# RWKV-7 recurrence with a gated mixture of experts: chunks of 64 steps on two diagonal 64x64 blocks of the array, in place of chunks of 128 steps

## The chip, the cores and the metric

One NeuronCore of one Trainium2 chip runs the kernel. The metric is the device time in microseconds (us), the median of several runs; a profiled execution of the same program gives the trace. TensorE's granted clock is shown by the trace as a share of full speed: 1.00 is 2.4 GHz and 0.50 is 1.2 GHz.

## The reference, cut to what matters

```python
# r, k, v, w, a, b: (4 batches, 8 heads, 768 steps, 40), float32
for t in range(S):                       # 768 steps, one after the other
    y[:, :, t] = einsum('bhd,bhde->bhe', rt, state)
    Sa = einsum('bhde,bhe->bhd', state, at)
    state = state * wt[:, :, None, :] - outer(Sa, bt) + outer(vt, kt)
x = y as (3072 tokens, 320)              # 4 x 768 tokens, 8 heads x 40
# two-level gate: argmax of 4 groups, then of 4 experts in the group
# out[token] = gate weight * (relu(x @ w1[expert]) @ w2[expert])
# w1: 16 experts of 320 x 1024; w2: 16 experts of 1024 x 320
```

## The kernel before, in words

The kernel has three stages. The recurrence makes the tokens (L157 to L376). The gate (L452 to L598) ranks the tokens by expert. The expert network (L601 to L681) gathers the tokens of each of 16 experts, multiplies by both weight matrices and scatters the result.

The recurrence cuts the 768 steps into 6 chunks of 128. A **unit** (L192) is one chunk of one batch with all 8 heads, so there are 24 units. Heads lie in pairs: the 40 rows of an even head on partitions 0 to 39, those of an odd head on partitions 64 to 103 (`blk`, L189). Within a unit the decay products are scanned (L218), inverted (L222) and multiplied into a, b and k (L224 to L226). `product` (L236) makes the 128x128 matrices GT, E, MT and NT of each head from 40-row operands; `natural` (L228) transposes on TensorE. The solve with the unit triangular matrix I+E runs in 7 levels (L281): in each, E and its transpose are squared for each head (L287, L296; 128x128 weights, 128 columns), and the 40 columns of U are multiplied (L307; 128x128 weights, 40 columns). ScalarE and VectorE copy each result from PSUM (L290, L300, L302, L313). Then follow the new state (L328 to L332, L356), the output (L342 to L351), its transpose and the gate logits (L135, L146).

Everything is float32. A matmul call on float32 stands in the trace as two records, each with a weight load of its own. The instructions of each engine run in the order that a list scheduler writes at build time: it takes the earliest instruction in program order whose inputs and buffers are ready, by its own cost table, so that work of the next unit is put where an earlier one waits. Inputs are held in three buffers (`NB = 3`). PSUM has five slots of one bank ("big") and three ("small"). A guard at the end (L368 to L379) sets the trip count of a step-by-step loop, which is zero here. Two expert weight buffers are filled during the recurrence (`WE = 2`), and a third exists from the expert stage on.

Of the kernel before, what the change touches and what calls it, by code (L numbers as in the profile page):

```python
# [9 lines left out]
F32 = mybir.dt.float32  # L10
# [11 lines left out]
W_MIN, W_MAX, T_MAX = 0.765, 1.3, 1.0  # L22
# [3 lines left out]
def kernel(  # L26
# [19 lines left out]
    C = P  # L46
    NC = S // C
    NN = B * NC
    NP = H // 2
    HW = 64  # L50
# [13 lines left out]
    LEVELS = C.bit_length() - 1  # L64
# [7 lines left out]
    psum = ctx.enter_context(tc.tile_pool(name="ps", bufs=1, space=PSUM))  # L72

    def big(shape):
        return psum.tile(shape, F32, tag="big", name="big", bufs=5)

    def small(shape):
        return psum.tile(shape, F32, tag="small", name="small", bufs=3)
# [13 lines left out]
    up4 = up[:, None, :].broadcast_to([P, NP, P])  # L92
    low4 = low[:, None, :].broadcast_to([P, NP, P])

# [3 lines left out]
    wg = cpool.tile([P, NK, NW], F32, name="wg")  # L98
    for ko, (k0, kn) in enumerate(KO):
        nc.scalar.dma_start(out=wg[:kn, ko, :G], in_=w_group[k0:k0 + kn, :])  # L100
        nc.scalar.dma_start(out=wg[:kn, ko, G:].rearrange("p (g e) -> p g e", g=G),
                            in_=w_expert[:, k0:k0 + kn, :].rearrange("g p e -> p g e"))
# [3 lines left out]
    WE = 2  # L106
# [20 lines left out]
    t_sum = cpool.tile([P, NN, H], F32, name="t_sum")  # L127
    w_max = cpool.tile([P, NN], F32, name="w_max")
    w_min = cpool.tile([P, NN], F32, name="w_min")
# [11 lines left out]

    def gate_logits(pool, xn, n):
        t = transpose_x(pool, xn)
        ps = small([P, NW])
        for ko, (_, kn) in enumerate(KO):
            nc.tensor.matmul(ps, lhsT=t[:kn, ko, :], rhs=wg[:kn, ko, :],  # L146
                             start=(ko == 0), stop=(ko == NK - 1))
        nc.scalar.copy(out=lg[:, n, :], in_=ps)

    with ExitStack() as part:  # L157
        pers = part.enter_context(tc.tile_pool(name="pers", bufs=1))
        sb = part.enter_context(tc.tile_pool(name="sb", bufs=2))

        NB = 3
        ins = []
        for i in range(NB):
            d = {}
            for nm in "wakbvr":
                d[nm] = pers.tile([P, NP, C], F32, name=f"in_{nm}{i}")
            d["pq"] = pers.tile([P, NP, C + 1], F32, name=f"pq{i}")
            ins.append(d)
        zeros = pers.tile([P, C], F32, name="zeros")
        nc.vector.memset(zeros, 0.0)  # L170
        U_pad = []
        for i in range(2):
            t = pers.tile([P, H, HW], F32, name=f"U{i}")
            nc.gpsimd.memset(t[:, :, D:], 0.0)
            U_pad.append(t)


        ST, SN = [], []
        for b_ in range(B):
            t = pers.tile([P, NP, 2, HW], F32, name=f"ST{b_}")  # L180
            nc.gpsimd.memset(t, 0.0)
            ST.append(t)
            SN.append(pers.tile([P, NP, 2, HW], F32, name=f"SN{b_}"))
        own = pers.tile([P, 2], F32, name="own")
        nc.gpsimd.memset(own, 0.0)
        for j in range(2):
            nc.gpsimd.memset(own[j * HW:(j + 1) * HW, j:j + 1], 1.0)

        def blk(h):  # L189
            return slice((h % 2) * HW, (h % 2) * HW + D)  # L190

        for u in range(NN):  # L192
            c, b_ = divmod(u, B)
            n = b_ * NC + c
            t0 = c * C
            d = ins[u % NB]
            if u < NB:

                for nm in "wakbvr":
                    for q0 in (32, 96):  # L200
                        nc.any.memset(d[nm][q0:q0 + 32], 1.0 if nm == "w" else 0.0)  # L201
                nc.any.memset(d["pq"][:, :, 0:1], 1.0)
            if NB < u <= NB + WE:
                load_weights(u - NB - 1, wbuf[u - NB - 1])
            for nm, src in (("w", wT), ("a", aT), ("b", bT), ("k", kT), ("r", rT), ("v", vT)):
                sv = src[b_, :, :, t0:t0 + C].rearrange("(i j) d t -> j d i t", j=2)
                for j in range(2):
                    nc.sync.dma_start(out=d[nm][j * HW:j * HW + D], in_=sv[j])
            vn = sb.tile([P, H, D], F32, name="vn")
            nc.sync.dma_start(out=vn, in_=v[b_, :, t0:t0 + C, :].rearrange("h t d -> t h d"))  # L210


            nc.vector.tensor_reduce(out=w_max[:, n:n + 1], in_=d["w"], axis=AX.XY, op=ALU.max)
            nc.vector.tensor_reduce(out=w_min[:, n:n + 1], in_=d["w"], axis=AX.XY, op=ALU.min)
            nc.vector.tensor_scalar(d["w"], d["w"], W_MIN, W_MAX, op0=ALU.max, op1=ALU.min)
            pq = d["pq"]
            for i in range(NP):
                nc.vector.tensor_tensor_scan(pq[:, i, 1:], d["w"][:, i, :], zeros, 1.0,  # L218
                                             op0=ALU.mult, op1=ALU.add)
            Pm, Qm = pq[:, :, :C], pq[:, :, 1:]  # L220
            Qi = d["w"]
            nc.vector.reciprocal(out=Qi, in_=Qm)  # L222
            At, Kt, Bt, Rt, Vt = d["a"], d["k"], d["b"], d["r"], d["v"]
            nc.vector.tensor_tensor(At, At, Pm, op=ALU.mult)  # L224
            nc.gpsimd.tensor_tensor(Bt, Bt, Qi, op=ALU.mult)
            nc.gpsimd.tensor_tensor(Kt, Kt, Qi, op=ALU.mult)  # L226

            def natural(src, name, scale):  # L228
                pt = big([P, NP, P])
                for i in range(NP):  # L230
                    nc.tensor.transpose(pt[:, i, :], src[:, i, :], ident)
                t = sb.tile([P, NP, P], F32, name=name)
                nc.scalar.mul(t, pt, scale)
                return t

            def product(lhs, rhs, g, mask, name, bufs):  # L236
                ps = big([P, NP, P])
                for q in range(NP):
                    nc.tensor.matmul(ps[:, q, :], lhsT=lhs[blk(g), q, :], rhs=rhs[blk(g), q, :],  # L239
                                     start=True, stop=True)  # L240
                t = sb.tile([P, NP, P], F32, name=name, bufs=bufs)
                nc.vector.tensor_tensor(t, ps, mask, op=ALU.mult)  # L242
                return t


            GR = range(2)
            GT = [product(Kt, At, g, up4, "GT", 4) for g in GR]

            E = [product(At, Bt, g, low4, "E", 6) for g in GR]
            ET = []  # L250
            for g in GR:
                ts = t_sum[:, n, g * NP:(g + 1) * NP]
                nc.vector.tensor_reduce(out=ts, in_=E[g], axis=AX.X, op=ALU.add,
                                        apply_absolute_value=True)
                fit = sb.tile([P, NP, 1], F32, name="fit")
                nc.vector.tensor_scalar(fit[:, :, 0], ts, T_MAX, None, op0=ALU.max)  # L256
                nc.vector.reciprocal(out=fit, in_=fit)
                nc.gpsimd.tensor_tensor(E[g], E[g], fit.broadcast_to([P, NP, P]), op=ALU.mult)  # L258
                pt = big([P, NP, P])
                for i in range(NP):  # L260
                    nc.tensor.transpose(pt[:, i, :], E[g][:, i, :], ident)
                t = sb.tile([P, NP, P], F32, name="ET", bufs=6)
                nc.scalar.copy(out=t, in_=pt)
                ET.append(t)
            MT = [product(Vt, Rt, g, up4, "MT", 4) for g in GR]
            nB = natural(Bt, "nB", -1.0)
            Kn = natural(Kt, "Kn", 1.0)
            Pn = natural(Pm, "Pn", 1.0)


            ps = small([P, H, D])
            for i in range(NP):
                if c:
                    nc.tensor.matmul(ps[:, 2 * i:2 * i + 2, :], lhsT=At[:, i, :],
                                     rhs=ST[b_][:, i, :, :D], start=True, stop=False)
                for j in range(2):
                    nc.tensor.matmul(ps[:, 2 * i + j, :], lhsT=GT[j][:, i, :], rhs=vn[:, 2 * i + j, :],  # L277
                                     start=(c == 0), stop=(c == 0 or j == 1))
            U = sb.tile([P, H, D], F32, name="U", bufs=3)
            nc.scalar.copy(out=U, in_=ps)  # L280
            for lv in range(LEVELS):  # L281
                if lv:
                    E2, ET2 = [], []
                    for g in GR:
# [7 lines left out]
                        if lv == LEVELS - 1:  # L292
                            continue
# [415 lines left out]
```

## Time and profile before

| | us |
|---|---|
| median of 3 runs (2051.61 to 2067.24) | 2060.82 |
| the profiled execution: its own time | 2059.22 |
| its span, first to last instruction | 2057.5 |
| its mean granted TensorE clock | 0.795 |
| VectorE busy in the span | 635.0 |
| ScalarE busy in the span | 411.5 |

The span is read in stages: a lead-in without a matmul, the recurrence, the gate, the experts. PE is the matmul queue and PEld its weight loads, DVE is VectorE, ACT ScalarE, POOL GpSimd, SP the queue that issues most transfers. A matmul record of shape 128*128 has weights of 128 rows and 128 columns; "128x40" behind it is the operand that streams, 128 rows and 40 columns. The ends of matmul records are modelled, so the distance between starts is the better price.

### The profile page before, as it was taken

The page shows a single profiled execution, that of the slowest core. Times are in us where ns is not written, and L with a number is a line of the kernel's source. Part 1 is how long each engine was busy: PE and PEld are TensorE (multiplying, and loading weights), DVE is VectorE, ACT ScalarE, POOL GpSimd, SP SyncE. Part 2 cuts the span into 40 slices and gives each one's busy share as a digit, 9 for nine tenths or more (in the row PEclk, how much of TensorE's full clock was granted, in tenths as well). Part 3 has the DMA queues.
Part 4 walks back from the last instruction along what each step waited for, and adds up shares of the span by engine and source line. Part 5 has one row for each costly group of instructions (what it writes and reads, how often), then busy time and mean ns, then how long its engine had stood idle before and what let it go on. Part 6 is the DMA issues. An engine that isn't in the chain of part 4 may idle for free. (4 is left out here: it accounts for less than half of the span.)

```text
span 2057.5 us, 29577 instructions
## 1 busy us (share of the span) xinstructions
PE 1942.0 (94%) x12542; PEld 1820.6 (88%) x12542; DVE 635.0 (31%) x1113; ACT 411.5 (20%) x755; POOL 194.7 (9%) x196
## 2 busy tenths in 40 slices
PE   5999999999999999999999999999999937999997
PEld 5999999999999999999999999999999936777776
DVE  8433332332334233323332333233221251111111
ACT  3122222212222122122221221122112200000000
POOL 3000000000000000000000000000000002121210
PEclk9787788758878688588786886687677858999999
DMA  5200000000000000000000000000000003444430
GB/s 142 64 20 20 26 23 14 17 26 16 18 20 27 15 22 17 27 18 18 17 26 20 17 17 23 14 20 17 10 4 1 4 5 133 153 160 153 159 128 11
DMA packets 104553, 84.59 MB, mean 41 GB/s; under 512 B 31961, under 2 KB 97502, under 8 KB 104416
## 3 DMA queue, kind: packets, MB, share of 16 engines
q1 hardware_dynamic: 99648, 73.42, 11.9%
q0 software_dynamic: 3072, 9.18, 1.1%
q8 instruction: 102, 1.67, 0.3%
q10 hardware_dynamic: 1696, 0.03, 0.0%
q14 instruction: 35, 0.29, 0.0%
HBM read 74.74 MB, written 9.18 MB: 41 GB/s over the span
## 5 line engine op out<-in xcount | busy, mean ns | idle before, releaser
L307 PE MATMUL small<-U,ET 128*128 128x40 f32 x2688 | 345.9, 290 | 0.6 <-ACT ET L290 0.4
L307 PEld LDWEIGHTS small<-U,ET 128*128 128x128 f32 x2688 | 341.1, 205 | 2.3 <-ACT ET L290 0.5
L287 PE MATMUL big<-ET,E 128*128 128x128 f32 x2304 | 335.8, 292 | 0.1
L287 PEld LDWEIGHTS big<-ET,E 128*128 128x128 f32 x2304 | 299.7, 203 | 0.2 <-DVE E L302 0.2
L296 PE MATMUL big<-E,ET 128*128 128x128 f32 x1920 | 265.8, 284 | 0.0
L290 ACT COPY ET<-big 128x512 f32<-128x512 f32 x288 | 168.7, 586 | 481.3 <-PE big L287 481.3
L296 PEld LDWEIGHTS big<-E,ET 128*128 128x128 f32 x1920 | 247.1, 201 | 0.0
L313 DVE TENSOR_TENSOR U<-U,small 128x320 f32<-128x320 f32 x168 | 80.7, 480 | 457.5 <-PE small L307 457.5
L633 PE MATMUL big<-xT,w1s 128*128 128x256 f32 x768 | 171.4, 383 | 10.3 <-DVE xT L626 10.3
L633 PEld LDWEIGHTS big<-xT,w1s 128*128 128x128 f32 x768 | 145.6, 191 | 34.2 <-DVE xT L626 14.8
L258 POOL TENSOR_TENSOR E<-E,fit 128x512 f32<-128x512 f32 x48 | 48.9, 1039 | 1189.5 <-DVE fit L256 1137.8
L642 PE MATMUL small<-w2s,hT 128*128 128x320 f32 x512 | 140.4, 432 | 0.0
L642 PEld LDWEIGHTS small<-w2s,hT 128*128 128x128 f32 x512 | 97.3, 190 | 38.8
L239 PE MATMUL big<-in_a,in_k 40*128 40x128 f32 x384 | 89.0, 447 | 17.1 <-DVE in_b L201 17.1
L348 PE MATMUL small<-nB,NT 128*128 128x40 f32 x384 | 100.2, 356 | 0.0
L239 PEld LDWEIGHTS big<-in_a,in_k 40*128 40x128 f32 x384 | 75.1, 322 | 26.9 <-POOL in_k L226 17.1
L302 DVE COPY E<-big 128x512 f32<-128x512 f32 x96 | 66.2, 691 | 100.1 <-PE big L296 98.5
L346 PE MATMUL small<-Kn,MT 128*128 128x40 f32 x384 | 96.0, 344 | 0.0
L300 ACT COPY E<-big 128x512 f32<-128x512 f32 x144 | 84.3, 585 | 50.4 <-PE big L296 50.4
L277 PE MATMUL small<-vn,GT 128*128 128x40 f32 x384 | 94.1, 402 | 0.0
L277 PEld LDWEIGHTS small<-vn,GT 128*128 128x128 f32 x384 | 91.8, 333 | 0.9 <-DVE E L242 0.7
L348 PEld LDWEIGHTS small<-nB,NT 128*128 128x128 f32 x384 | 87.7, 281 | 2.3 <-DVE NT L242 2.3
(189 smaller groups left out, 2064.2 us busy)
## 6 DMA issues: line engine op xcount, KB each, us to landing
w2s<-in_w_dram SPq DMA_DIRECT2D x16, 1280.0 KB
w1s<-in_w_dram SPq DMA_DIRECT2D x16, 1024.0 KB
w1s<-in_w_dram SPq DMA_DIRECT2D x16, 256.0 KB
vn<-in_v_dram SPq DMA_DIRECT2D x24, 160.0 KB
in_w<-in_wT_dram SPq DMA_DIRECT2D x48, 80.0 KB
in_a<-in_aT_dram SPq DMA_DIRECT2D x48, 80.0 KB
in_b<-in_bT_dram SPq DMA_DIRECT2D x48, 80.0 KB
in_k<-in_kT_dram SPq DMA_DIRECT2D x48, 80.0 KB
```

What stands on the lines that cost most here:

```text
L239: nc.tensor.matmul(ps[:, q, :], lhsT=lhs[blk(g), q, :], rhs=rhs[blk(g), q, :], start=True, stop=True)
L277: nc.tensor.matmul(ps[:, 2 * i + j, :], lhsT=GT[j][:, i, :], rhs=vn[:, 2 * i + j, :], start=(c == 0), stop=(c == 0 or j == 1))
L287: nc.tensor.matmul(ps[:, q, :], lhsT=E[g][:, q, :], rhs=ET[g][:, q, :], start=True, stop=True)
L290: nc.scalar.copy(out=t, in_=ps)
L296: nc.tensor.matmul(ps[:, q, :], lhsT=ET[g][:, q, :], rhs=E[g][:, q, :], start=True, stop=True)
L300: nc.scalar.copy(out=t, in_=ps)
L307: nc.tensor.matmul(ps[:, h, :], lhsT=ET[h % 2][:, h // 2, :], rhs=U[:, h, :], start=True, stop=True)
L313: nc.vector.tensor_tensor(nx, U, ps, op=ALU.add if lv else ALU.subtract)
L346: nc.tensor.matmul(o, lhsT=MT[j][:, i, :], rhs=Kn[:, i, blk(j)], start=(c == 0), stop=False)
L348: nc.tensor.matmul(o, lhsT=NTm[j][:, i, :], rhs=nB[:, i, blk(j)], start=False, stop=(c == 0 or j == 1))
L633: nc.tensor.matmul(ps[:, f, :], lhsT=w1s[:, ko, (f0 + f) * P:(f0 + f + 1) * P], rhs=xT[:, ko, :w], start=(ko == 0), stop=(ko == NK - 1))
L642: nc.tensor.matmul(ps, lhsT=hT[:, f, t_ * P:(t_ + 1) * P], rhs=w2s[:, f, :], start=(f == 0), stop=(f == FQ - 1))
```

## The change

The recurrence is rewritten; the gate and the experts stay. A unit is now one chunk of 128 steps of two batches (12 units), and each unit holds two chunks of 64 steps (24 chunks), one after the other. A chunk treats 8 head pairs (`NI`) at once. Each matmul of a chunk uses a 64x64 block of the array: rows and columns 0 to 63 for an even head, 64 to 127 for an odd head, issued in turn (`each`). Both heads of a pair write the same PSUM bank, on partitions 0 to 63 and 64 to 127. There are 6 levels in place of 7; they form the inverse itself (`ED`'s right half, then `DT`) and no longer carry U. U is then DT times the right-hand side. The state is updated every 64 steps and scaled by the decay product every 128. The output is formed transposed (`yT`). The decay scan runs over four head pairs at once, the reciprocal over 8. PSUM is cut into two "wide" slots of two banks and four slots of one bank. Two sums of squares on ScalarE take the place of the clamp of w in the guard. Input buffers are two (`NB = 2`, each of twice the size), and one expert weight buffer is filled early (`WE = 1`).

Left out of the diff below, in the order of the program, calls of a chunk, each on a 64x64 block with 64 columns or fewer: 16 for E (At by Bt), 16 for MT (Vt by Rt); in level 0, 16 for ED's left half and 16 for the square of E; in level 4, 16 for ED's right half and 16 for the square; in level 5, 16 for DT; after the right-hand side (RHS) 16 for U (DT by RHS), 32 for the state (GK by vn, TBt by U), 16 each for UT, NTm and Sn. At the end of a unit stand, for each of its two batches, 4 transposes of yT and 4 gate matmuls with yT as weights, all with 128x128 weights.

```diff
+    HW = P // 2
+    L = 2 * HW
+    NS = 2
+    BS = B // NS
+    NI = BS * NP
-    LEVELS = C.bit_length() - 1
+    LEVELS = HW.bit_length() - 1
-    WE = 2
+    WE = 1
...
+            return psum.tile([P, NI, 2 * HW], F32, tag="wide", name="wide", bufs=2)
...
+            for i in range(NI):
+                for j in range(2):
+                    yield i, j
...
+            nc.vector.reciprocal(out=Qi, in_=pq[:, :, 1:])
+            junk = sb.tile([P, NI, L + 1], F32, name="junk", bufs=1)
+            nc.scalar.activation(junk, pq, ACT.Square, accum_out=q_sum[:, 2 * u:2 * u + 1])
...
+                for lhs, out_t, mask in ((Kt, GK, m_gk), (Bt, TBt, m_tb)):
+                    ps = wide()
+                    for i, j in each():
+                        nc.tensor.matmul(ps[half(j), i, :HW + D], lhsT=lhs[half(j, D), i, ts],
+                                         rhs=At[half(j, D), i, c2, :HW + D], start=True, stop=True)
+                    nc.vector.tensor_tensor(out_t[:, :, :HW + D], ps[:, :, :HW + D], over(mask),
+                                            op=ALU.mult)
...
+                for lv in range(LEVELS):
...
+                    elif lv < LEVELS - 2:
+                        ps = wide()
+                        for i, j in each():
+                            nc.tensor.matmul(ps[half(j), i, :], lhsT=E[half(j), i, :],
+                                             rhs=ED[half(j), i, :], start=True, stop=True)
+                        nxt = sb.tile([P, NI, 2 * HW], F32, name="ED", bufs=3)
+                        nc.scalar.copy(out=nxt[:, :, :HW], in_=ps[:, :, :HW])
+                        nc.vector.tensor_tensor(nxt[:, :, HW:], ps[:, :, HW:], ED[:, :, HW:], op=ALU.add)
...
+                    if not last:
+                        ps = bank([P, NI, HW], "one", 2)
+                        for i, j in each():
+                            nc.tensor.matmul(ps[half(j), i, :], lhsT=ET[half(j), i, :],
+                                             rhs=E[half(j), i, :], start=True, stop=True)
+                        E = sb.tile([P, NI, HW], F32, name="E", bufs=3)
+                        nc.scalar.copy(out=E, in_=ps)
...
+                ps = bank([P, NI, D], "seq", 2)
+                for i, j in each():
+                    nc.tensor.matmul(ps[half(j), i, :], lhsT=GK[half(j), i, :HW], rhs=vn[half(j), c2, i, :],
+                                     start=True, stop=fresh)
+                    if not fresh:
+                        nc.tensor.matmul(ps[half(j), i, :], lhsT=At[half(j, D), i, c2, :HW],
+                                         rhs=S0[half(j, D), i, :D], start=False, stop=True)
+                nc.scalar.copy(out=RHS[:, :, :D], in_=ps)
...
+                ps = bank([P, NI, HW], "one", 2)
+                for i, j in each():
+                    if not fresh:
+                        nc.tensor.matmul(ps[half(j), i, :], lhsT=Sn[half(j, D), i, :],
+                                         rhs=Rt[half(j, D), i, ts], start=True, stop=False)
+                    nc.tensor.matmul(ps[half(j), i, :], lhsT=GK[half(j), i, HW:], rhs=MT[half(j), i, :],
+                                     start=fresh, stop=False)
+                    nc.tensor.matmul(ps[half(j), i, :], lhsT=TBt[half(j), i, HW:], rhs=NTm[half(j), i, :],
+                                     start=False, stop=True)
+                nc.vector.tensor_tensor(yT[:, :, ts], ps, Pm[:, :, ts], op=ALU.mult)
```

## Rows read from the trace of the kernel before

**Rows 1.** The page: busy time of each engine; granted clock in 40 slices.
```profile
PE 1942.0 (94%) x12542; PEld 1820.6 (88%) x12542; DVE 635.0 (31%) x1113; ACT 411.5 (20%) x755; POOL 194.7 (9%) x196
PEclk9787788758878688588786886687677858999999
```

**Rows 2.** Windows by stage; columns PE, PEld, DVE, ACT, POOL busy, clock, DMA share, GB/s.
```profile
0.00:17.08 17.08, 0.00 (x1) 0.00 (x1) 14.26 (x24) 12.55 (x20) 9.53 (x25) 1.00 0.50 124
...
400.00:1600.00 1200.00, 1176.90 (x8134) 1139.21 (x8133) 377.46 (x642) 267.99 (x484) 78.77 (x64) 0.75 0.07 18
...
1660.50:1717.85 57.35, 15.95 (x70) 12.56 (x70) 25.79 (x75) 1.49 (x7) 9.74 (x16) 0.56 0.18 61
```

**Rows 3.** Windows between four changes of the granted clock; columns as in Rows 2.
```profile
740.00:768.38 28.38, 27.62 (x245) 27.00 (x243) 6.12 (x13) 7.92 (x14) 0.00 (x0) 1.00 0.04 7
768.38:788.86 20.48, 20.07 (x101) 18.64 (x102) 7.00 (x16) 3.22 (x7) 2.04 (x2) 0.50 0.12 36
788.86:822.99 34.13, 33.55 (x301) 33.40 (x300) 13.70 (x20) 11.14 (x20) 2.94 (x2) 1.00 0.05 13
822.99:867.37 44.38, 43.80 (x216) 41.85 (x215) 15.88 (x26) 6.47 (x13) 4.98 (x4) 0.50 0.11 29
```

**Rows 4.** Timeline at clock 1.00: start, duration, engine, line, operands, shapes, count.
```profile
803.17 1.06 PE L287 MATMUL big<-ET,E 128*128 128x128 f32 x8
...
804.06 1.06 PE L296 MATMUL big<-E,ET 128*128 128x128 f32 x8
...
804.95 1.88 PE L307 MATMUL small<-U,ET 128*128 128x40 f32 x16
...
806.66 1.14 PE L287 MATMUL big<-ET,E 128*128 128x128 f32 x8
```

**Rows 5.** Timeline at clock 0.50, two row blocks in turn.
```profile
773.41 0.42 PE L239 MATMUL big<-in_a,in_k 40*128 40x128 f32 x1
...
773.57 0.42 PE L239 MATMUL big<-in_b,in_a 40*128 40x128 f32 x1
...
773.62 0.42 PE L239 MATMUL big<-in_a,in_k 40*128 40x128 f32 x1
...
773.79 0.42 PE L239 MATMUL big<-in_b,in_a 40*128 40x128 f32 x1
...
773.83 0.42 PE L239 MATMUL big<-in_a,in_k 40*128 40x128 f32 x1
```

**Rows 6.** Timeline at clock 0.50, full blocks with few columns, 24 records in all.
```profile
776.22 0.71 PE L274 MATMUL small<-ST,in_a 128*128 128x80 f32 x2
776.73 0.99 PE L277 MATMUL small<-vn,GT 128*128 128x40 f32 x4
...
781.36 1.95 PE L261 MATMUL big<-ident,E 128*128 128x128 f32 x8
```

**Rows 7.** Groups by line and shape: busy us, mean ns of one | idle before.
```profile
L307 PE MATMUL small<-U,ET 128*128 128x40 f32 x2688 | 345.9, 290 | 0.6 <-ACT ET L290 0.4
...
L624 PEld LDWEIGHTS big<-ident,xt 128*128 128x128 f32 x64 | 8.6, 145 | 13.1 <-issue 9.1 <-DMA xt<-x_nat,src_i 0.9
...
L624 PEld LDWEIGHTS big<-ident,xt 128*64 128x64 f32 x32 | 3.7, 115 | 0.0
```

**Rows 8.** Groups by line and shape, other engines.
```profile
L290 ACT COPY ET<-big 128x512 f32<-128x512 f32 x288 | 168.7, 586 | 481.3 <-PE big L287 481.3
...
L222 DVE RECIPROCAL in_w<-pq 128x512 f32<-128x512 f32 x24 | 80.5, 3353 | 0.8
...
L226 POOL TENSOR_TENSOR in_k<-in_k,in_w 128x512 f32<-128x512 f32 x24 | 39.5, 1648 | 0.0
```

**Rows 9.** Timelines: two matmuls that wait for a copy, idle time in brackets.
```profile
759.66 0.66 PE L318 MATMUL big<-ident,U 128*128 128x128 f32 x4 [0.58 <-DVE U L313]
...
1649.31 3.09 PE L239 MATMUL big<-in_r,UT 40*128 40x128 f32 x16 [0.68 <-ACT UT L321]
```

**Rows 10.** Window in which an expert's weights land; columns as in Rows 2.
```profile
1710.00:1720.00 10.00, 3.93 (x11) 2.70 (x12) 0.85 (x2) 0.52 (x2) 4.82 (x6) 0.52 0.92 322
```

More of the change, by code (lines that the diff above doesn't have):

```diff
@@ L16 @@
 DRAM = bass.MemoryType.DRAM
-W_MIN, W_MAX, T_MAX = 0.765, 1.3, 1.0
+Q_MAX, T_MAX = 1e30, 1.0
 @with_exitstack
@@ L45 @@
     DM = H * D
-    C = P
-    NC = S // C
+    HW = P // 2
+    L = 2 * HW
+    NC = S // L
+    NP = H // 2
+    NS = 2
+    BS = B // NS
+    NI = BS * NP
+    CH = NS * NC * 2
     NN = B * NC
-    NP = H // 2
-    HW = 64
     G, Eg = w1.shape[0], w1.shape[1]
@@ L71 @@
     dpool = ctx.enter_context(tc.tile_pool(name="dram", bufs=1, space=DRAM))
[L72 to L78, printed above, removed]
     ident = cpool.tile([P, P], F32, name="ident")
@@ L91 @@
                             pattern=[[-1, P]], channel_multiplier=1)
-    up4 = up[:, None, :].broadcast_to([P, NP, P])
-    low4 = low[:, None, :].broadcast_to([P, NP, P])
     x_nat = dpool.tile([NTOK, DM], F32, name="x_nat")
     lg = cpool.tile([P, NN, NW], F32, name="lg")
[L98 to L102, printed above, removed]
-    WE = 2
+    wgp = cpool.tile([P, NP, NW], F32, name="wgp")
+    nc.gpsimd.memset(wgp, 0.0)
+    for j in range(2):
+        rows = slice(j * HW, j * HW + D)
+        nc.scalar.dma_start(out=wgp[rows, :, :G],
+                            in_=w_group.rearrange("(i j d) g -> j d i g", j=2, d=D)[j])
+        for g in range(G):
+            nc.scalar.dma_start(out=wgp[rows, :, G + g * Eg:G + (g + 1) * Eg],
+                                in_=w_expert[g].rearrange("(i j d) e -> j d i e", j=2, d=D)[j])
+    WE = 1
     KR = KO[-1][1]
@@ L131, in transpose_x, with big, small @@
+    psum = ctx.enter_context(tc.tile_pool(name="ps", bufs=1, space=PSUM))
+    def big(shape):
+        return psum.tile(shape, F32, tag="big", name="big", bufs=5)
+    def small(shape):
+        return psum.tile(shape, F32, tag="small", name="small", bufs=3)
     def transpose_x(pool, src):
@@ L444 @@
         with tc.For_i(0, n_back, 1):
+            wg = sq.tile([P, NK, NW], F32, name="wg")
+            for ko, (k0, kn) in enumerate(KO):
+                nc.scalar.dma_start(out=wg[:kn, ko, :G], in_=w_group[k0:k0 + kn, :])
+                nc.scalar.dma_start(out=wg[:kn, ko, G:].rearrange("p (g e) -> p g e", g=G),
+                                    in_=w_expert[:, k0:k0 + kn, :].rearrange("g p e -> p g e"))
             for n in range(NN):
@@ L447 @@
                 nc.sync.dma_start(out=xn, in_=x_nat[n * P:(n + 1) * P, :])
-                gate_logits(sq, xn, n)
+                t = transpose_x(sq, xn)
+                ps = small([P, NW])
+                for ko, (_, kn) in enumerate(KO):
+                    nc.tensor.matmul(ps, lhsT=t[:kn, ko, :], rhs=wg[:kn, ko, :],
+                                     start=(ko == 0), stop=(ko == NK - 1))
+                nc.scalar.copy(out=lg[:, n, :], in_=ps)
     with ExitStack() as part:
```

419 lines of the change are left out of this document (209 added, 210 removed).

## The prediction

> **What bounds the kernel now.** I read the page first. TensorE is busy 94% of the span, VectorE 31%, ScalarE 20% [rows 1]. The windows by stage say where: in the 1200 us from 400 on, TensorE is busy 1177, so only 2% is idle, at a mean granted clock of 0.75 [rows 2]. So the recurrence is bound by TensorE's own records; nearly every wait of the other engines is cover. The lead-in without a matmul takes 17.08 us, and gate and experts take 2057.5 - 1660.5 = 397 us, of which only the first weights change [rows 2].
>
> The mean clock of 0.75 hides two levels. From 740 to 768.38 us the clock stands at 1.00, then 20.5 us at 0.50, 34.1 at 1.00, 44.4 at 0.50 [rows 3]. TensorE is busy in all of them (20.07 of 20.48, 43.80 of 44.38), so a busy engine alone doesn't hold the clock up. What differs is what it does: at 1.00 it streams full 128x128 blocks, most of them with 128 columns [rows 4]; in the 0.50 stretches lie the 40-row products [rows 5] and full blocks that stream only 40 or 80 columns [rows 6].
>
> Three prices come from distances between starts. At 1.00, 8 records with 128 columns take 0.89 us, 111 ns each, and 16 records with 40 columns take 1.71 us, 107 ns each [rows 4]. So with 128 weight columns, few streamed columns save nothing. At 0.50, 24 records with 40 or 80 columns take 5.14 us, 214 ns each [rows 6]. And two products on different row blocks, issued in turn, overlap: starts at 773.41, 773.57, 773.62, 773.79, 773.83 are two records per 0.21 us at 0.50, the time of one [rows 5].
>
> **The change part by part.** One old unit and one new chunk are the same share of the work, 24 of each. A call is two records 8 heads x 7 levels x 24 units x 2 = 2688 [rows 7]. When calls alternate between the two blocks, the second record of one runs beside the first of the next, so a call costs one step. I take the clock at 0.50 (reasons below).
>
> The price of a 64-column step isn't in the trace. It lies between 107 ns at 0.50, half of the 128-column step, and 214 ns, no saving. The nearest row: a weight load of 64 columns takes 115 ns where one of 128 takes 145 [rows 7], 30 ns less for 64 columns, which is about a column per 2.4 GHz clock. So I take the proportional price: 107 ns up to 64 columns, 174 for 104, 214 for 128.
>
> A chunk then has:
> - GK and TB: 32 calls with 104 columns, 5.6 us.
> - Levels 1 to 3, the double-width products: 48 calls with 128 columns, 10.3 us.
> - Calls with at most 64 columns that alternate (E, MT, the other level products, DT, U, UT, NTm, Sn): 224 x 107 ns = 24.0 us.
> - Groups in which the calls of one head follow each other on the same block: RHS and state, 64 calls, three steps for two; y, 48 calls, five steps for three. 96 + 80 = 176 steps, 18.8 us.
> - Transposes and gate calls: 16 calls, 32 records of 214 ns per unit, 3.4 us per chunk.
>
> That is 62.1 us, times 24 = 1490; two chunks without state save 17 us and the last two, without a state update, 10: **1463 us**. What it removes is the old 1643 us from 17.08 to 1660.5.
>
> Idle time comes on top. A chunk has 11 hand-offs in which TensorE needs a copy of what it has just made: E, five squares, DT, RHS, U, UT, NTm. Uncovered, one costs 0.58 to 0.68 us [rows 9], so 7.5 us per chunk, 180 in all. One reciprocal over 1024 columns blocks VectorE's queue for 2 x 3.35 = 6.7 us [rows 8], and the level's add behind it, for which TensorE waits: 12 x 6.7 = 80. With nothing covered the recurrence takes 1463 + 260 = 1723; covered as now (2% idle) 1463 / 0.98 = 1493. The next chunk's GK, TB, E and MT (9 us) need nothing from the levels and can cover them, but two wide and two single PSUM slots serve both. I take a quarter of the way, **1550**.
>
> ScalarE's copies (13 per chunk) of at most 586 ns [rows 8], about 8 us, hide beside 62 us of TensorE, and so do the two sums of squares; were ScalarE the bound, the recurrence would take under 300 us.
>
> The lead-in grows: the reciprocal doubles (+3.35) and so does the product with k on GpSimd (+1.65) [rows 8], and the scans; 17 becomes 23. The last chunk's end has no next chunk to cover it: +10. A unit's loads (2240 KB, 18 us at the lead-in's 124 GB/s [rows 2]) queue on SP, and behind them the stores of x; with two input buffers they have a whole unit, over 120 us, to land: nothing. If that cover failed, each unit would pay up to 18 us. `WE = 1` moves one expert's load (2.56 MB, 8 us at the 322 GB/s of [rows 10]) into the time of expert 0, 339.65 / 16 = 21 us: nothing; without that cover 8 us per expert.
>
> Sum: 23 + 1550 + 10 + 397 = 1980 of span. The profiled execution takes 1.7 us more than its span (2059.22 against 2057.5), and the median is 1.6 above that run: I forecast **1982 us**. A 1% difference, some 20 us, is about what a measurement of this kernel can tell from none.
>
> **Why the half clock.** In the stretches at 1.00 full 128x128 blocks prevail; two 64x64 blocks together fill half of its cells, with the 40-row operands less. The nearest rows are the 40-row pairs [rows 5]: two blocks overlap, the engine doesn't pause, and the clock stays at 0.50. But those blocks have all 128 columns and few rows, the new ones 64 of each; the trace has no stretch of blocks with half the columns, so whether unused columns count like unused rows is open.
>
> The Trainium skill, TensorE: Matmul & The Clock Gate, Part 1, says that a busy engine releases the throttle and an idle one brings it back. By that rule the new recurrence would run at 1.00, which is the first rival below; the trace speaks against the plain rule, since the engine is busy 43.80 of 44.38 us at 0.50.
>
> **The rivals.**
> - *Full clock.* The steps halve to 732 us, the hand-offs don't: 747 to 992, and half the way, since less work covers the same hand-offs, is 870. With 430 around it and 1.7, **1302** (1179 to 1424). For it: the 64-row work keeps both row halves of the array fed. Against it: [rows 5].
> - *The two blocks don't overlap.* Each call pays two steps: 11.1 + 20.5 + 47.9 + 24.0 + 3.4 = 107 us per chunk, 2532 after the savings, 2584 with 2% idle, **3015** at the half clock. Against it: the row blocks overlap now [rows 5], though into different PSUM tiles and on all columns. It decides for slower once about a seventh of the overlap is lost: the time before leaves (2059 - 432) / 24 = 68 us per chunk, between 61 and 105.
> - *The chain of hand-offs sets the pace.* Nothing covered at the half clock: 1723 + 432 = **2155**. It decides for slower when over 164 of the 260 us stay uncovered. For it: one chunk has one chain, where a unit had two groups of heads to alternate. Against it: the present 2% idle.
> - *The change doesn't do what it says*: the guard starts the step loop, or the scheduler mixes streams so that calls on the same block follow each other. The first would cost far more than the whole recurrence.
>
> The Trainium skill, TensorEngine Tiling (Array Packing), Gotcha 1, speaks against this change: different row tiles can't use the same PSUM bank at once, and both heads of a pair write one bank. By that rule the second rival's 3015 would come. No row here shows it either way; the same page says that tiles work independently, and the two heads write different partitions of the bank.
>
> **How the numbers follow.** Half clock with overlap has 0.56; its own range is 1758 (the scheduler slips other calls between those of the accumulating groups, 64 steps or 6.8 us per chunk less, and 2% idle) to 2155. Of it 0.40 lies under 2040, 0.08 within 1%, 0.08 above, which is the chain rival. Full clock has 0.29, no overlap 0.09, the rest 0.06 (0.02 faster, 0.01 same, 0.03 slower). So faster 0.71, same 0.09, slower 0.20. The range from 1250 to 2160 leaves out no overlap, most of the rest and a little of the full clock.
>
> **What would show it.** Clock about 0.50 through the recurrence, back to 1.00 with the experts. Starts of the level calls 107 ns apart per call, the two blocks a few ns apart. TensorE idle about 5%, before E's and DT's readers. First matmul near 23 us, last part 397. Wrong at once if the clock stands at 1.00 (then near 1300), if calls lie 214 ns apart (then near 3000), or if the levels wait for VectorE behind the reciprocal.

## The result and the profile after

The changed kernel takes **1312.28 us** (median of 4 runs, 1311.65 to 1312.87) against 2062.16 (4 runs, 2051.61 to 2067.24): a ratio of 0.637, interval 0.634 to 0.639. The forecast was 1982 with a range from 1250 to 2160. The sign was right, the size wrong by 670 us. What came is the first rival, the full clock, priced at 1302.

The profiled execution takes 1312.87 us, its span 1311.2. Its page, first the busy time of each engine and then the granted clock in 40 slices, answers to [rows 1]:

```profile
PE 1124.4 (86%) x21366; PEld 1023.2 (78%) x21366; DVE 440.0 (34%) x560; ACT 253.6 (19%) x485; POOL 180.1 (14%) x155
...
PEclk9898989999898989989898998999579999999999
```

TensorE's records went from 12542 to 21366, and their busy time fell from 1942 us to 1124. The clock's row holds the answer: 8 and 9 through the recurrence, where a row of 5 was forecast. The dip at slices 29 and 30 is the stretch between recurrence and experts, which was at a low clock before, too.

Windows by stage (columns as in [rows 2]): the recurrence, what lies between it and the experts, the experts.

```profile
24.74:912.00 887.26, 790.19 (x19912) 757.58 (x19912) 344.00 (x369) 209.73 (x398) 94.80 (x47) 0.94 0.14 37
912.00:975.00 63.00, 18.15 (x94) 14.76 (x93) 25.77 (x74) 2.49 (x9) 10.47 (x16) 0.59 0.20 64
975.00:1311.20 336.20, 316.11 (x1364) 250.81 (x1362) 49.69 (x94) 26.85 (x62) 57.73 (x58) 0.99 0.41 134
```

The recurrence takes 887.26 us where it took 1643, the lead-in 24.74 (forecast 23), the rest 63.00 + 336.20 = 399.2 (forecast 397). So the whole error lies in the recurrence.

Its clock is 0.94, again a mean of two levels. Windows between three changes of the clock, over one unit of two chunks (columns as in [rows 2]):

```profile
568.98:633.80 64.82, 58.62 (x1572) 55.97 (x1569) 25.16 (x27) 14.97 (x29) 2.53 (x2) 1.00 0.14 38
633.80:644.00 10.20, 8.39 (x120) 8.24 (x122) 4.26 (x6) 2.90 (x5) 5.64 (x2) 0.50 0.12 34
```

A period of 75 us holds 64.8 at 1.00 and 10.2 at 0.50. The timeline shows the price of a call at each level. At 1.00:

```profile
570.05 1.96 PE L300 MATMUL wide<-ED,E 64*64 64x128 f32 x32 [0.68 <-ACT E L322]
571.84 1.10 PE L319 MATMUL one<-E,ED 64*64 64x64 f32 x32
...
629.98 0.34 PE L335 MATMUL seq<-ST,At 40*64 40x40 f32 x4
630.10 0.34 PE L332 MATMUL seq<-vn,GK 64*64 64x40 f32 x4
630.21 0.34 PE L335 MATMUL seq<-ST,At 40*64 40x40 f32 x4
```

and at 0.50, around the change of unit:

```profile
631.61 0.34 PE L335 MATMUL seq<-ST,At 40*64 40x40 f32 x4
634.83 1.97 PE L293 MATMUL one<-TB,E 64*64 64x64 f32 x32 [2.88 <-DVE E L272]
636.59 1.92 PE L319 MATMUL one<-E,TB 64*64 64x64 f32 x32
639.28 3.68 PE L300 MATMUL wide<-ED,E 64*64 64x128 f32 x32 [0.78 <-ACT E L322]
642.72 1.72 PE L319 MATMUL one<-E,ED 64*64 64x64 f32 x32
```

Here 32 records are 16 calls of two records. At 1.00, 16 calls of 128 columns take 571.84 - 570.05 = 1.79 us, 112 ns each. At 0.50 they take 642.72 - 639.28 = 3.44, 215 ns each, and 16 calls of 64 columns 636.59 - 634.83 = 1.76, 110 ns each. The forecast's prices at 0.50 were 214 and 107. So **two blocks overlap fully, a call costs one step, and from 64 to 128 streamed columns the price is proportional to them**, all as forecast; only the level of the clock is another. The accumulating groups, forecast at three steps for two calls, cost one each: the scheduler put L332 of one head between L335 of another, two calls (4 records) every 0.115 us, 58 ns a call.

The last timeline also shows what the engine did before the clock fell: it stood still for 2.88 us, from 631.95 to 634.83, waiting for E of the unit that starts there; the clock fell at 633.80. VectorE was busy meanwhile:

```profile
627.68 6.55 DVE L244 RECIPROCAL Qi<-pq 128x1024 f32<-128x1024 f32 x1
634.14 0.63 DVE L272 TENSOR_TENSOR E<-one,low_n 128x512 f32<-128x512 f32 x1
```

The multiplication of E by its mask queues behind the reciprocal that the unit after that one needs. The waits of TensorE (in us: total, number, longest) put a sum to it:

```profile
PE wide L300 <- ACT E L322: 38.5, 58, 0.8
PE one L293 <- DVE E L272: 29.7, 10, 3.9
...
PE one L394 <- DVE yT L385: 9.4, 12, 0.8
PE one L379 <- ACT Sn L375: 8.2, 12, 0.7
```

Most of the recurrence adds up from these prices. The steps of the forecast with one step for every call, a single record for each transpose and the prices of 1.00 are 29.1 us a chunk, 24 x 29.1 = 698, some 10 less for chunks without a state or an update: 688. Each product behind which TensorE has to wait ends with a tail (1.96 us of busy time where 1.79 lie to the next start); it waits 110 times, 110 x 0.17 = 19. A mean clock of 0.94 in 887 us is 106 us at 0.50, busy for 8.39 / 10.20 of it, and half of that is lost: 44. The first 11.7 us, ahead of the first change of the clock that the trace holds, at 36.48, ran at 0.50 too by their records, though the clock's column reads 1.00 there: 6 more. Together these estimates make 757 of the 790.19 us busy; 33 aren't accounted for. Idle are 887.26 - 790.19 = 97 us, most of them the four waits above.

### The profile page after: what moved, and what is told of

The parts are those of the page before. It is cut to its first block, busy times and chain, and to the rows that moved or that the text cites. A ratio compares the mean times of both kernels' runs of the same rounds, so it can differ in the third digit from the quotient of the medians.

```text
span 1311.2 us, 45533 instructions
## 1 busy us (share of the span) xinstructions
PE 1124.4 (86%) x21366; PEld 1023.2 (78%) x21366; DVE 440.0 (34%) x560; ACT 253.6 (19%) x485; POOL 180.1 (14%) x155
## 5 line engine op out<-in xcount | busy, mean ns | idle before, releaser
L300 PE MATMUL wide<-ED,E 64*64 64x128 f32 x2304 | 158.5, 293 | 38.9 <-ACT E L322 38.5
L300 PEld LDWEIGHTS wide<-ED,E 64*64 64x64 f32 x2304 | 140.2, 145 | 47.8 <-ACT E L322 36.3
L319 PE MATMUL one<-E,ED 64*64 64x64 f32 x3072 | 112.0, 225 | 0.0
L319 PEld LDWEIGHTS one<-E,ED 64*64 64x64 f32 x3072 | 108.8, 142 | 0.0
L322 ACT COPY E<-one 128x512 f32<-128x512 f32 x120 | 70.2, 585 | 108.3 <-PE one L319 107.9
L244 DVE RECIPROCAL Qi<-pq 128x1024 f32<-128x1024 f32 x12 | 78.6, 6553 | 0.4
L263 PE MATMUL wide<-At,in_k 40*64 40x104 f32 x768 | 50.9, 255 | 24.7 <-POOL in_k L251 24.7
L379 PE MATMUL one<-in_r,Sn 40*64 40x64 f32 x704 | 64.8, 221 | 8.2 <-ACT Sn L375 8.2
L379 PEld LDWEIGHTS one<-in_r,Sn 40*64 40x64 f32 x704 | 61.8, 132 | 9.9 <-ACT Sn L375 9.9
L381 PE MATMUL one<-MT,GK 64*64 64x64 f32 x768 | 68.2, 218 | 0.0
L383 PE MATMUL one<-NTm,TB 64*64 64x64 f32 x768 | 67.8, 218 | 0.0
L381 PEld LDWEIGHTS one<-MT,GK 64*64 64x64 f32 x768 | 65.9, 134 | 0.0
L383 PEld LDWEIGHTS one<-NTm,TB 64*64 64x64 f32 x768 | 65.7, 135 | 0.0
```

The source lines that it names most:

```text
L244: nc.vector.reciprocal(out=Qi, in_=pq[:, :, 1:])
L263: nc.tensor.matmul(ps[half(j), i, :HW + D], lhsT=lhs[half(j, D), i, ts], rhs=At[half(j, D), i, c2, :HW + D], start=True, stop=True)
L300: nc.tensor.matmul(ps[half(j), i, :], lhsT=E[half(j), i, :], rhs=ED[half(j), i, :], start=True, stop=True)
L319: nc.tensor.matmul(ps[half(j), i, :], lhsT=ET[half(j), i, :], rhs=E[half(j), i, :], start=True, stop=True)
L322: nc.scalar.copy(out=E, in_=ps)
L379: nc.tensor.matmul(ps[half(j), i, :], lhsT=Sn[half(j, D), i, :], rhs=Rt[half(j, D), i, ts], start=True, stop=False)
```

## The experiments

Theory A, after the result: blocks that alternate between the two row halves keep all 128 rows fed, unused columns don't matter for the clock, and the short falls come from the reciprocal. Theory B: the clock goes by the share of the array's cells that is in use, columns as well as rows, and half of the cells, as the pairs use them, was enough. Theory C: the gain is fewer steps alone, and the overlap has little part in it. The kernels *blocks apart*, *reciprocal in pieces*, *halves* and *turns before* compute the whole reference; the two kernels of stretches compute none of it, only calls on a constant block, and write those.

**Blocks apart.** All calls of one head half first, then those of the other:

```
 def each():
-    for i in range(NI):
-        for j in range(2):
+    for j in range(2):
+        for i in range(NI):
             yield i, j
```

> The kernel after, with all calls of the even heads of a group ahead of those of the odd heads, so that neighbouring calls use the same 64x64 block. Theory (two blocks side by side overlap and, with both row halves fed, hold 2.4 GHz; unused columns of the array don't count): a call costs two steps, 107 to 116 ns in place of 58 at 1.00, so at least 1266 us of steps in the recurrence, a span near 1800 if the clock holds at 1.00, and up to 2900 where the clock falls to 0.50 because only one row half is fed. Rival A (a 64x64 call is cheap by itself, the overlap gives nothing): about 1312, as after. Rival B (any busy TensorE holds the clock): near 1800 with a mean clock over 0.9.

It takes 2587.55 us (one run), slower than before the change, and within what theory A gave for a fallen clock. Groups by line and shape of this kernel:

```profile
L300 PE MATMUL wide<-ED,E 64*64 64x128 f32 x2304 | 452.4, 421 | 30.7 <-ACT E L322 30.7
```

and the same group of the changed kernel, the first line over the whole span, then in 569 to 633 us at 1.00 and in 634 to 644 us at 0.50:

```profile
L300 PE MATMUL wide<-ED,E 64*64 64x128 f32 x2304 | 158.5, 293 | 38.9 <-ACT E L322 38.5
...
L300 PE MATMUL wide<-ED,E 64*64 64x128 f32 x160 | 9.8, 272 | 2.6 <-ACT E L322 2.6
...
L300 PE MATMUL wide<-ED,E 64*64 64x128 f32 x32 | 3.7, 420 | 0.8 <-ACT E L322 0.8
```

A record of 421 ns is one at 0.50. (The clock's own column reads 1.00 in this run up to 2227 us, ahead of the first change of the clock that the trace holds. That change is a rise to 1.00, and records of 421 ns say 0.50 before it; so the level is read from the records here.) Order alone, with the same calls, is worth 2587.55 - 1312.28 = 1275 us: most of the overlap goes, and the clock too. That rules out theory C. This kernel can't say how much each is worth; the stretches below price it.

**Stretches.** Calls of one kind, some 20 to 35 us each, on fixed blocks; four of them behind 40 calls on the full array (`warm`):

```
for q in range(warm):
    nc.tensor.matmul(ps[q % 2][:, :128], lhsT=W[:, :128], rhs=x[:, :128], start=True, stop=True)
for q in range(calls):
    j = where[q % len(where)]                # the half of the array
    r = slice(64 * j, 64 * j + rows)
    o = ps[j if banks == 2 else 0]           # PSUM tile; oc, c: the place in it
    ...
    nc.tensor.matmul(o[oc, c:c + n], lhsT=W[r, 128:128 + cols], rhs=x[r, :n],
                     start=True, stop=True)
```

> Matmul calls alone: eleven stretches of one kind of call each, none of the reference computed, only some rows of the output written. Between stretches TensorE stands still for some 20 us; four stretches begin with 40 calls on the full array. Theory: clock from a standstill: sa (one 64x64 block) stays at 0.50 with 214 ns a call; sb (two blocks in turn, 64 rows, one PSUM bank) rises to 1.00 with 58 ns a call; sc (the same, two banks) as sb; sd (two blocks, 40 rows) stays at 0.50 with 107 ns; se (two row blocks of 40 rows, 128 columns) stays at 0.50 with 214 ns; sf (64 rows, 128 columns, in turn) rises to 1.00 with 111 ns; sg (one row block of 64 rows, 128 columns) stays at 0.50 with 427 ns. After full calls at 1.00: si (two blocks, 40 rows) and sj (40 rows, 128 columns, in turn) stay at 1.00, sh (one block, 64 rows) perhaps, sk (one block, 40 rows) falls to 0.50. Rival A, the forecast (unused columns count like unused rows): sb, sc, sd stay at 0.50, only sf rises, si falls. Rival B (any busy TensorE holds the clock): all rise to 1.00 within some us. Rival C (one PSUM bank for two row blocks serializes): sb takes 107 to 116 ns a call where sc takes 58.

The pauses of some 20 us ahead of the stretches didn't come about: from sb on TensorE waited at most 1.31 us, so the clock of one stretch reached into the next, and sc ran in part with one block's calls behind the other's (28.56 us for its 640 records, where sb took 21.30). What can be read of the first seven agrees with the theory in the level of the clock: sb and sf (64-row blocks in turn, 64 and 128 columns) rose to 1.00; sa and sg (one block; sa by its records, 34.39 us / 320 = 107 ns), se and most of sd (40-row blocks) stood at 0.50. The four behind 40 full 128x128 calls started at 1.00, and the timeline shows whether they kept it (at 1.00 a record takes 58 ns with 64 columns and 112 with 128, and half of that with two blocks in turn):

```profile
242.95 18.88 PE L84 MATMUL sh<-xsh,W 64*64 64x64 f32 x320
...
270.88 18.88 PE L84 MATMUL si<-xsi,W 40*64 40x64 f32 x640
...
298.82 18.14 PE L84 MATMUL sj<-xsj,W 40*128 40x128 f32 x320
...
326.85 30.12 PE L84 MATMUL sk<-xsk,W 40*64 40x64 f32 x320
```

One block of 64 rows (sh), two of 40 rows with 64 columns (si) and two of 40 rows with 128 columns (sj) kept 1.00 to their end; one block of 40 rows (sk) fell to 0.50 and took 30.12 us for what sh did in 18.88. So in these stretches of some 18 us a clock that was up stayed up with calls (si, sj, sh) with which it didn't come up in the next kernel (tf, tg, th). That isn't safe: sd, the same calls as si, started at 1.00 behind sc and a wait of 1.18 us, and fell to 0.50 at 110.17, 2.3 us after its start.

**Stretches with pauses.** Such stretches with some 19 us of pause ahead of each and the blocks strictly in turn.

> Matmul calls alone, ten stretches, each after a pause of some 20 us that all calls wait for and with the calls strictly in turn; none of the reference computed, only some rows of the output written. Theory (rows fed count for the clock, unused columns don't): ta (two 64x64 blocks, one bank), tb (the same, two banks), tc (two blocks of 64 rows and 32 columns), td (one block of 128 rows and 64 columns) and te (128 rows, 32 columns) all rise to 1.00 in the first third; tf (two blocks, 40 rows, 64 columns), tg (two row blocks, 40 rows, 128 columns) and th (one block of 64x64) stay at 0.50. Prices at 1.00: ta and tb 58 ns a call, at 0.50 in tf 107, tg 213, th 213. Rival A, the forecast (cells in use count): tg, with 0.62 of the cells, rises before ta (0.50) or td (0.50), and tc and te (0.25) never rise. Rival C (one bank for two row blocks serializes): ta takes twice tb's time. Open, told apart by ti (all four 64x64 blocks in turn): 58 ns a call if blocks on the same rows exclude each other, 29 ns if all four run at once.

Timeline of six of the ten stretches (records counted; two are one call):

```profile
22.64 24.93 PE L74 MATMUL ta<-xta,W 64*64 64x64 f32 x800 [22.64 <-DVE xta L68]
...
203.91 28.25 PE L74 MATMUL te<-xte,W 128*32 128x64 f32 x480 [19.20 <-DVE xte L68]
251.36 34.40 PE L74 MATMUL tf<-xtf,W 40*64 40x64 f32 x640 [19.20 <-DVE xtf L68]
304.96 34.51 PE L74 MATMUL tg<-xtg,W 40*128 40x128 f32 x320 [19.20 <-DVE xtg L68]
358.74 34.36 PE L74 MATMUL th<-xth,W 64*64 64x64 f32 x320 [19.27 <-DVE xth L68]
...
457.62 42.90 PE L74 MATMUL tj<-xtj,W 64*64 64x40 f32 x800 [18.67 <-DVE xtj L68]
```

Windows within ta, tb, tc, td, te, tf, tg, th and tj, in this order, TensorE alone (busy, records, clock, DMA share, GB/s):

```profile
30.00:47.00 17.00, 17.00 (x590) 1.00 0.02 5
75.00:91.00 16.00, 16.00 (x556) 1.00 0.02 4
120.00:135.00 15.00, 15.00 (x545) 1.00 0.02 4
163.00:184.00 21.00, 21.00 (x364) 1.00 0.01 2
213.00:231.00 18.00, 18.00 (x327) 1.00 0.01 3
255.00:285.00 30.00, 30.00 (x569) 0.50 0.01 2
310.00:339.00 29.00, 29.00 (x275) 0.50 0.00 1
363.00:392.00 29.00, 29.00 (x275) 0.50 0.00 1
460.00:500.00 40.00, 40.00 (x756) 0.50 0.01 2
```

All nine are busy for the whole of their window. Five went up to 1.00: two 64x64 blocks in one PSUM tile (ta) or in two (tb), two 64x32 blocks (tc), one 128x64 block (td), one 128x32 block (te), all of which feed the 128 rows and stream 64 columns. At 0.50 stayed two blocks of 40 rows with 64 columns (tf) or with all 128 (tg), and one block of 64 rows (th). The pair that decides against theory B is te and tg: te uses a quarter of the cells and went up, tg uses 80 of 128 rows on all columns, 0.62 of them, and stayed. Theory B falls: among these stretches the array's columns in use made no difference to the granted clock, and ta and tf, or sf and tg, differ in nothing but the rows.

But theory A doesn't hold as it stands either. tj has the two 64x64 blocks of ta in turn, feeds all 128 rows, was busy for 40.00 of 40.00 us, and stayed at 0.50. It differs from ta in streaming 40 columns instead of 64. So feeding all rows wasn't enough here, and what the clock goes by stays open.

The Trainium skill, TensorE: Matmul & The Clock Gate, Part 1, has a busy engine release the throttle. The first five stretches agree; tf, tg, th and tj, busy for all of 29 to 40 us at 0.50, don't, and the measurement decides.

The prices: two 64x64 blocks in turn take 17.00 us / 590 = 29 ns a record at 1.00, 58 a call; at 0.50 the 40-row pair takes 30.00 / 569 = 53 ns, 105 a call. One block by itself takes 105 ns a record at 0.50 (th, 29.00 / 275), 211 a call, and 59 at 1.00 (sh, 18.88 / 320), 118 a call. So overlap is worth a factor of two at either clock, and the clock another two. tb takes 16.00 us / 556, also 29 ns a record: both heads of a pair in one PSUM bank cost nothing. Gotcha 1 of the Trainium skill's page TensorEngine Tiling (Array Packing), by which different row tiles can't use one bank at once, doesn't hold for these two blocks, which differ in their columns too.

**Turns before.** The kernel before, with only its products of 40 rows issued in turn for the two groups of heads:

```
-def product(lhs, rhs, g, mask, name, bufs):
-    ps = big([P, NP, P])
+def product(lhs, rhs, mask, name, bufs):
+    pss = [big([P, NP, P]) for g in range(2)]
     for q in range(NP):
-        nc.tensor.matmul(ps[:, q, :], lhsT=lhs[blk(g), q, :], rhs=rhs[blk(g), q, :], ...)
+        for g in range(2):
+            nc.tensor.matmul(pss[g][:, q, :], lhsT=lhs[blk(g), q, :], rhs=rhs[blk(g), q, :], ...)
```

> The kernel before, with one part of the change alone: the 40-row products issued for the two heads of a pair in turn, into two PSUM banks, in place of one row block after the other. Theory (row blocks in turn overlap): of the 16 records of a product 7 or 8 are hidden, 28 to 32 steps of 107 to 214 ns per unit, 72 to 160 us in all, and a little more where the clock then falls later; 1900 to 1990. Rival (the overlap is there already through the order that the scheduler writes, or PSUM slots make the pairs wait): within 20 us of 2060.

It takes 1973.96 us (4 runs, 1969.64 to 1979.03), a ratio of 0.958, interval 0.954 to 0.963: 87 us less. The group of the last product, first in the kernel before, then in this one:

```profile
L239 PE MATMUL big<-in_r,UT 40*128 40x128 f32 x384 | 61.8, 380 | 2.7 <-ACT UT L321 2.7
```

```profile
L240 PE MATMUL big<-in_r,UT 40*128 40x128 f32 x384 | 34.4, 330 | 2.7 <-ACT UT L325 2.7
```

The same 384 records occupy 34.4 us of the engine instead of 61.8: the overlap that [rows 5] showed happened only where the scheduler put two products in turn by itself. The other three products fall by 20.8, 24.4 and 28.1 us. So the overlap has a value without the new algorithm, 87 us, small beside the 750 of the whole change.

**Reciprocal in pieces.** The changed kernel with the reciprocal in 8 pieces of 128 columns, so that the mask of E can pass between two of them:

```
-nc.vector.reciprocal(out=Qi, in_=pq[:, :, 1:])
+for i in range(NI):
+    nc.vector.reciprocal(out=Qi[:, i, :], in_=pq[:, i, 1:])
```

> The kernel after, with the reciprocal over 1024 columns cut into eight of 128. Theory (the reciprocal of 6.55 us in VectorE's queue makes TensorE wait about 2.9 us once per unit, the clock falls for 10.2 us behind it, which costs some 5 us more): the short stretches at 0.50 vanish, the wait of L293 for E goes from 29.7 us to under 5, and the time falls by 60 to 90 us, to 1220 to 1250. Rival (the wait just moves: the products with the reciprocal on GpSimd, or VectorE's total work, set the start of the next chunk): within 15 us of 1312.

It takes 1242.41 us (4 runs, 1239.78 to 1251.06), a ratio of 0.604 to the kernel before, interval 0.600 to 0.607: 70 us less than the changed kernel. Window from 100 to 800 us, first of the changed kernel, then of this one:

```profile
100.00:800.00 700.00, 620.84 (x15535) 594.85 (x15533) 282.06 (x291) 167.72 (x320) 79.28 (x38) 0.93 0.14 37
```

```profile
100.00:800.00 700.00, 648.18 (x17245) 621.28 (x17246) 302.76 (x387) 181.47 (x351) 81.86 (x40) 1.00 0.14 37
```

The stretches at 0.50 behind the changes of unit are gone, and so is the wait for E of its line L293. The sum of the two, 44 + 29.7 = 74, is about the 70 us measured. So in the changed kernel the reciprocal's pauses of 2 to 4 us caused the falls of the clock, as theory A has it.

**Halves.** The same with the copy of E's square in two halves, so that the next level can start on the first:

```
-nc.scalar.copy(out=E, in_=ps)
+for i0 in (0, NI // 2):
+    nc.scalar.copy(out=E[:, i0:i0 + NI // 2], in_=ps[:, i0:i0 + NI // 2])
```

> The kernel with the reciprocal in eight pieces, and also the copy of each square of E out of PSUM cut into two halves of four head pairs. Theory (what is left of TensorE's idle time is the hand-off to the next level, 36 us behind the copy of E): the next level starts behind the first half, some 0.27 us earlier per uncovered hand-off, 48 of them: 10 to 20 us below the kernel with the reciprocal in pieces, 1222 to 1232. Rival (two copies of 256 columns take longer than one of 512 and delay ScalarE's other copies, or the second half is waited for): within 6 us of 1242, or above.

It takes 1230.05 us (5 runs, 1227.1 to 1236.67), a ratio of 0.596, interval 0.594 to 0.599: 12 us less. The wait that it aims at, first in *reciprocal in pieces*, then here:

```profile
PE wide L301 <- ACT E L323: 36.2, 48, 1.3
```

```profile
PE wide L301 <- DVE ED L305: 11.4, 24, 0.6
...
PE wide L301 <- ACT E L324: 8.3, 13, 1.1
```

36.2 us fall to 8.3, and the other operand, which VectorE adds, comes late for 11.4: net 16 us, of which 12 are seen in the medians. This is the fastest version, 82 us below the changed kernel.

Its clock isn't steady, though. In the profiled execution (1236.67 us, the slowest of the five) it fell five times before 800 us, for 41 us in all, each time at the end of a unit, though TensorE had waited for no more than 0.8 us at a time in the 8 us before. The longest wait ahead of one of them, and the window from that fall to the rise:

```profile
701.56 0.66 PE L396 MATMUL one<-ident,yT 128*128 128x128 f32 x4 [0.78 <-DVE yT L387]
```

```profile
704.43:714.67 10.24, 10.24 (x188) 10.24 (x186) 7.92 (x11) 2.37 (x6) 1.69 (x1) 0.50 0.06 19
```

So a pause of 2 to 4 us isn't the only thing that such a fall follows; what caused these stays open.

## Why the prediction was wrong in its size

**The step that failed** is the one under "Why the half clock", carried into the sum as "I take the clock at 0.50". It took the 40-row pairs of [rows 5] as the nearest rows and let the unused columns of the 64x64 blocks weigh like their unused rows. The text itself called this open. The runs showed the other answer: the recurrence stood at 1.00 in 64.8 of 75 us, te rose with a quarter of the cells, and tg stayed down with 0.62 of them. [rows 5] differ from the new calls in both respects, rows and columns, and among the stretches with 64 or more streamed columns the one that told was the rows, 40 instead of 64 (tf against ta). The reason given for the rival, that 64-row work keeps both row halves fed, fits these, but isn't all of it: tj feeds both halves and stayed at 0.50. So that the clock was up is measured, and that unused columns don't keep it down is shown; why this mix, in which some calls have 40 rows or stream 40 columns, comes up is not.

**What held.** The prices of the steps: 107 and 214 ns forecast at 0.50, 110 and 215 measured. That two blocks overlap: confirmed in the timeline, borne out by *blocks apart* and priced by the stretches. The lead-in, gate and experts, 23 + 397 forecast, 24.7 + 399.2 measured; `WE = 1` shows no wait that costs anything there (336.2 us for the experts, where the forecast went by 339.65), though no run undid it by itself. The reciprocal as a danger: named with 80 us, it cost about 70, by another way than named: 29.7 of waiting for E, not for the level's add, and the rest by the clock that fell in the wait.

**What was off beside the clock.** The accumulating groups: one step per call, not three for two, 64 steps a chunk fewer, 64 x 24 x 53 ns = 81 us at 1.00; half of that went again, since the steps cost 58 and 112 ns instead of 53.5 and 107. The transposes: a unit's 16 calls stand in the trace as 24 records, not 32, because each of the 8 transposes is one record (L394 has 96 in 12 units); 8 x 12 x 214 ns = 21 us too much in the sum, half of it at 1.00. The rival of 1302 took 732 us of steps and 138 of hand-offs; measured are 688 of steps, 19 of tails, 50 of low clock, 33 not accounted for and 97 idle, which is 887 against 870. Its closeness to 1312 thus rests partly on terms that cancel, and that part is luck. Hand-offs: L300 waits for its E in 58 of 72 products at up to 0.8 us, so the next chunk's independent work seldom covers that one; most of the others are covered, and the 97 us idle lie near the forecast's 1550 - 1463 = 87, though 29.7 of them are the reciprocal's. The forecast's last sum comes to 1980 + 1.7 + 1.6 = 1983, not 1982, which decides nothing.

**The rivals that didn't come.** No overlap was priced at 3015; the kernel built for it, *blocks apart*, took 2587.55. Its timeline shows where the price was too high:

```profile
1021.96 0.36 PE L293 MATMUL one<-TB,E 64*64 64x64 f32 x1
1022.06 0.31 PE L277 MATMUL one<-in_r,in_v 40*64 40x64 f32 x1
...
1024.64 0.36 PE L319 MATMUL one<-E,TB 64*64 64x64 f32 x1
```

A product of 16 calls takes 1024.64 - 1021.96 = 2.68 us, where the forecast went by 16 x 214 ns = 3.42: at the border the first block of the next product runs beside the second block of the last one, so a part of the overlap is left. Some 14 products a chunk with 0.74 us each make 10 of the 18 us by which a chunk is cheaper, (2588 - 1.7 - 25 - 399) / 24 = 90 against 2584 / 24 = 108; the three products of double width give more of the same kind. The chain of hand-offs doesn't set the pace: TensorE is busy for 790 of 887 us.

**Open.** How the 1275 us of *blocks apart* divide between overlap and clock in the kernel itself; whether the clock would have come up by these blocks if they hadn't alternated so strictly; why tj stayed at 0.50, and why the clock fell in *halves* without a long pause.

## What to carry to other kernels

Small blocks pay twice on this array if two of them on different row halves alternate call by call: they overlap, and in this kernel the clock came up to 1.00 with them as it did with full blocks, while the same calls block after block ran at half the clock and with little overlap. It isn't a rule: with 40 streamed columns instead of 64, a stretch of the same pairs stayed at 0.50. Before pricing work at a granted clock, look for a stretch of the trace that is like it in rows, in columns and in streamed columns; where none is, the level of the clock is an open factor of two, and the likeliest case should say so. Once the matrix engine is fast, look at the two or three microseconds that it waits at each change of unit: a long vector instruction queued ahead of the short one that the matrix engine needed cost 70 us of 1312, and cutting it in pieces gave them back.

## What the runs showed of the hardware beside this

- The same calls ran at either level, by what stood before them: two 40-row blocks in turn stayed at 1.00 for 18.88 us behind full calls (si), fell 2.3 us after their start behind a short wait (sd), and stayed at 0.50 for 34.40 us behind a pause (tf).
- After a wait of 2.88 us with the clock falling in it, the clock needed until 644.00, 9.2 us after the work went on, to come back.
- Four 64x64 blocks, all of the array's quarters in turn, ran at once: bursts of 128 records in 2.09 us, 16 ns each, but with idle gaps of 1.4 to 1.6 us between them for which the profile shows no releaser:

```profile
424.25 2.09 PE L74 MATMUL ti<-xti,W 64*64 64x64 f32 x128 [1.64 <-issue]
```

  With the gaps, a record takes 27 to 29 ns, hardly less than the 29 of two blocks; what the engine's instruction supply does there wasn't pursued.
- Few streamed columns saved nothing: two 64x64 blocks that stream 40 columns (tj) took 40.00 us for 756 records, 53 ns each, at 0.50, as much as the pair with 64 columns at that clock (tf).
